# Issuing each unit's value product half a unit later in a hashed-attention kernel with two feed-forward layers behind it

## The chip, the cores and the metric

The program runs on one core of one Trainium2 chip. The metric is device time in microseconds (us), the median of several executions; less is better. Six queues matter: PE (TensorE's matmuls, in the order of the program), DVE (VectorE), ACT (ScalarE), POOL (GpSimd), and SP, which issues the DMAs. Each engine runs its own instructions in a fixed order and waits on semaphores for the others.

## The reference

Three steps follow each other: an attention whose mask is a hash (a query sees only the keys in its bucket), a feed-forward layer with an ELU, and one with a squared ReLU.

```python
def _attn_ref(q, k, v, proj):                 # B=2, H=8, S=768, D=64
    ...
    mask = q_bucket[:, :, :, None] == k_bucket[:, :, None, :]
    scores = scale * np.matmul(q, k.transpose(0, 1, 3, 2))
    scores = np.where(mask, scores, -1000000000.0)
    scores = scores - np.max(scores, axis=-1, keepdims=True)
    attn = np.exp(scores)
    attn = attn / (np.sum(attn, axis=-1, keepdims=True) + 1e-09)
    return np.matmul(attn, v).astype(np.float32)

def _moe_ref(x, w_in, w_out):                 # 1536 x 512, d_ff = 2048
    h = x @ w_in
    g = np.where(h > 0.0, h, alpha * (np.exp(np.minimum(h, 0.0)) - 1.0))
    return (g @ w_out).astype(np.float32)

def _moe2_ref(x, w_in, w_out, s, b):
    h = x @ w_in
    r = np.maximum(h, 0.0)
    return ((s * (r * r) + b) @ w_out).astype(np.float32)
```

The weights arrive in 64-bit floats; the kernel takes them apart into pairs of 16-bit parts itself.

## The kernel before

**Units.** The attention is 96 units: batch b, chunk c of 128 queries (6 per batch), head h (8 per chunk), in this order, so that units 0 to 47 are batch 0. A unit u is a chain over all engines, and the text calls its links by these names:

- scores S(u), `u_s`, line 358: 4 matmuls on PE (128 x 768 scores in two 16-bit parts) into one of two PSUM buffers;
- softmax, `u_soft`: DVE clamps and takes the maximum (line 368), POOL (units 16 to 43) or DVE scales it (line 369), ACT takes the exponential (line 370);
- split, `u_split`: ACT copies the probabilities to 16 bits (line 389, tile ph), POOL subtracts for the low part (line 392), and SP issues a DMA that transposes both parts (line 394, pt<-ph);
- value product A(u), `u_av`, line 412: 18 matmuls on PE from the transposed tile pt into xacc.

After the eighth head of a chunk `u_norm` divides by the sum (DVE, lines 426 to 430), and a transposing DMA puts the chunk into x for the first layer. Units 0 to 15 go another way (a transpose on PE, line 379); the change doesn't reach them.

**Layers.** The first layer works through six blocks of 256 tokens: `up` (h, 16 times 12 matmuls of 128x256, line 531) and `down` (x2p, 4 times 48). Behind each h tile come an exponential on ACT (e, line 539), DVE steps (e, g, lines 546 and 548), a copy on ACT (gh, line 551) and a subtraction on POOL (gl, line 554). While it runs, its weights are still being taken apart: DVE joins words (lines 194 to 197, wa), ACT rounds (wih, then woh, line 188), DVE subtracts for the low part (wil, wol, line 204). Then the second layer follows: `up2` (h) and `down2` (y, line 775).

**Order.** Between matmul groups the first layer hands out credit, and for each half of 2.5 us (1.2 us at first) the generator `attention` moves on to its next yield, which is half a unit. One round of its loop issues the split of the unit before, then A(u), then S of the unit `lag` later (4 units, PT = 4 buffers for pt, later 5), yields, then issues the softmax and what `sched` holds for that unit (the loads and hash bits of batch 1 from unit 41 on), and yields again. So A(u) and S(u+4) stand together, and the layer's products stand on either side. What the program writes is a priority, not the last word: the framework's scheduler places each instruction on its engine's queue by its own timeline, so that the final order differs a little from the written one. Rings bound the chain: 3 buffers for the exponentials, 3 for ph, 4 for pt.

At the boundary of the batches (units 41 to 50) the keys and queries of batch 1 are split (line 260), transposed, hashed on PE (pbit, line 320), compared on DVE (bits, line 323), and their buckets made on PE (pone, line 333) and written by ACT (line 337); the values are split by ACT (line 303) and DVE (vv, line 304).

Of the kernel before, what the change touches and what calls it, by code (L numbers as in the profile page):

```python
# [18 lines left out]
PT = 4  # L19
# [48 lines left out]
def model_kernel(tc, q, k, v, proj, w_in, w_out, w_in2, w_out2, s2, b2, sel, pop, eye, out):  # L68
    nc = tc.nc
    B, H, S, D = q.shape  # L70
    NB = proj.shape[1]
    DM, DFF = w_in.shape
    C = S // 128
# [3 lines left out]
    NU = B * C * H  # L77
# [15 lines left out]
    with ExitStack() as base:  # L93
# [248 lines left out]
        U0 = BLOCKS1[0] * H  # L342

        def unit(u):
            b, r = divmod(u, C * H)
            c, h = divmod(r, H)
            return b, c, h, h // 2, h % 2

        sps, pf, pt, sums, xacc = ({} for _ in range(5))
# [12 lines left out]
        def u_soft(u):  # L362
            b, c, h, hp, j = unit(u)
            if h == 0:
                sums[b, c] = sml.tile([128, H], F32, tag="sum", name="sum")
            f = ring.take("p", [128, S], F32, "p")
            mx = sml.tile([128, 1], F32, tag="mx", name="mx")
            nc.vector.tensor_scalar(f, sps.pop(u), CLAMP, None, op0=ALU.min, op1=ALU.min, accum_out=mx)  # L368
            (nc.gpsimd if U0 <= u < MXP else nc.vector).tensor_scalar(mx, mx, sm / (SQ * SQ), 10.0 * LN2, op0=ALU.mult, op1=ALU.add)  # L369
            nc.scalar.activation(out=f, in_=f, func=ACTF.Exp, scale=-sm / (SQ * SQ), bias=mx,  # L370
                                 accum_out=sums[b, c][:, h:h + 1])
            pf[u] = f

        def u_split(u, eng):
            f = pf.pop(u)
            if u < FC * H:
                p = ps_p[0].tile([128, S], F32, tag="s", name="pT")
                for cc in range(C):
                    nc.tensor.transpose(p[:, 128 * cc:128 * cc + 128], f[:, 128 * cc:128 * cc + 128], ident)  # L379
                o = ring.take("pt", [128, S], F32, "pt")  # L380
                if eng == "act":
                    nc.scalar.activation(out=o, in_=p, func=ACTF.Copy)
                else:
                    nc.vector.tensor_copy(out=o, in_=p)
                pt[u] = o
                return
            t = ring.take("ph", [128, 2, S], F16, "ph")
            if eng == "act":
                nc.scalar.activation(out=t[:, 0, :], in_=f, func=ACTF.Copy)  # L389
            else:  # L390
                nc.vector.tensor_copy(out=t[:, 0, :], in_=f)
            nc.gpsimd.tensor_tensor(out=t[:, 1, :], in0=f, in1=t[:, 0, :], op=ALU.subtract)  # L392
            o = ring.take("pt", [128, 2 * C, 128], F16, "pt")
            nc.sync.dma_start_transpose(out=o, in_=t.rearrange("p x s -> p (x s)"))
            pt[u] = o

        def u_av(u):
            b, c, h, hp, j = unit(u)
            if h == 0:
                xacc[b, c] = ps_x.tile([128, H, D], F32, tag="x", name="xacc")  # L400
            acc = xacc[b, c][:, h, :]
            o = pt.pop(u)
            if u < FC * H:
                vv = raws[b, hp, "v"].rearrange("p h (c d) -> p h c d", d=D)
                for cc in range(C):
                    nc.tensor.matmul(acc, o[:, 128 * cc:128 * cc + 128], vv[:, j, cc, :],  # L406
                                     start=(cc == 0), stop=(cc == C - 1))
                return
            vv = vHL[b, hp]
            for z, (x, y) in enumerate(((0, 0), (0, 1), (1, 0))):  # L410
                for cc in range(C):
                    nc.tensor.matmul(acc, o[:, C * x + cc, :], vv[:, j, cc, y, :],  # L412
                                     start=(z == 0 and cc == 0), stop=(z == 2 and cc == C - 1))
# [9 lines left out]
        def u_norm(b, c):  # L423
            sm_, acc = sums.pop((b, c)), xacc.pop((b, c))
            rs = sml.tile([128, H], F32, tag="rs", name="rs")
            nc.vector.tensor_scalar(rs, sm_, 1e-9 * SPR, (1.0 if b * C + c < FC else SV) / SX, op0=ALU.add, op1=ALU.mult)
            rr = sml.tile([128, H, 1], F32, tag="rr", name="rr")
            nc.vector.reciprocal(out=rr, in_=rs.rearrange("p (h o) -> p h o", o=1))
            xf = ring.take("p", [128, H, D], F32, "xf")
            nc.vector.tensor_tensor(out=xf, in0=acc, in1=rr.to_broadcast([128, H, D]), op=ALU.mult)  # L430
            xh = per.tile([128, 2, H * D], F16, tag="xh", name="xh")
            fl = xf.rearrange("p h d -> p (h d)")
            if FC <= b * C + c < C:
                nc.scalar.activation(out=xh[:, 0, :], in_=fl, func=ACTF.Copy)
            else:
                nc.vector.tensor_copy(out=xh[:, 0, :], in_=fl)
            nc.gpsimd.tensor_tensor(out=xh[:, 1, :], in0=fl, in1=xh[:, 0, :], op=ALU.subtract)
            ch = b * C + c
            nc.sync.dma_start_transpose(out=xx[ch // 4][:, :, ch % 4 * 128:ch % 4 * 128 + 128], in_=xh.rearrange("p x d -> p (x d)"))
# [27 lines left out]
        done_chunks = [0]  # L467
        in_done = [0]
        nxt = {"s": 0, "av": 0, "soft": [], "split": [], "lag": LAG0}

        def may_step():
            u = nxt["av"]
            return u >= NU or blk_of[u // H][0] < in_done[0] + XB

        def attention():
            for i in range(-PRE, 0):
                for fn, a in sched.get(i, []):
                    fn(*a)
                yield
            while nxt["av"] < NU:  # L480
                if nxt["split"]:
                    u_split(nxt["split"].pop(0), SPLIT(nxt["s"]))
                u = nxt["av"]
                if u < nxt["s"] and u in pt and (nxt["s"] - u >= nxt["lag"] or nxt["s"] == NU):
                    u_av(u)
                    nxt["av"] += 1
                    if u % H == H - 1:
                        b, c, *_ = unit(u)
                        u_norm(b, c)
                        done_chunks[0] = b * C + c + 1  # L490
                u = nxt["s"]
                if u < NU and u - nxt["av"] < nxt["lag"]:
                    if u == U0:
                        ring.use(p=[unp], ph=[un3], pt=[ptp])
                        nxt["lag"] = PT
                    u_s(u)
                    nxt["s"] += 1
                    yield
                    u_soft(u)
                    nxt["split"].append(u)  # L500
                    for fn, a in sched.get(u, []):
                        fn(*a)
                yield
        att = attention()


# [473 lines left out]
```

## Time and profile before

| | us |
|---|---|
| median of 3 runs | 713.86 |
| the runs | 713.5 to 716.53 |
| the profiled execution, its own time | 715.27 |
| its span in the trace | 713.5 |
| PE busy | 659.6 (92%) |
| DVE busy | 516.6 (72%) |
| ACT busy | 417.2 (58%) |
| POOL busy | 272.7 (38%) |

The page divides the span in forty slices of 17.8 us. The first 75 us hold the hash bits of batch 0 and the first units, with PE often waiting. From 98 us on the first layer runs beside the attention; the last value product is at 397 us. Second-layer products begin at 476 us. PE's busy time counts pipelined matmuls, so a busy PE isn't a PE at its peak; what it waits for is read from the idle time in square brackets in front of an instruction in the timeline, with the name of what ended it.

### The profile page before, as it was taken

The page shows a single profiled execution, that of the slowest core. Times are in us where ns is not written, and L with a number is a line of the kernel's source. Part 1 is how long each engine was busy: PE and PEld are TensorE (multiplying, and loading weights), DVE is VectorE, ACT ScalarE, POOL GpSimd, SP SyncE. Part 2 cuts the span into 40 slices and gives each one's busy share as a digit, 9 for nine tenths or more (in the row PEclk, how much of TensorE's full clock was granted, in tenths as well). Part 3 has the DMA queues.
Part 4 walks back from the last instruction along what each step waited for, and adds up shares of the span by engine and source line. Part 5 has one row for each costly group of instructions (what it writes and reads, how often), then busy time and mean ns, then how long its engine had stood idle before and what let it go on. Part 6 is the DMA issues. An engine that isn't in the chain of part 4 may idle for free.

```text
span 713.5 us, 15214 instructions
## 1 busy us (share of the span) xinstructions
PE 659.6 (92%) x6192; PEld 504.0 (71%) x6192; DVE 516.6 (72%) x885; ACT 417.2 (58%) x687; POOL 272.7 (38%) x219
## 2 busy tenths in 40 slices
PE   2789869888887999999999999999999999999998
PEld 0368657676666777888888988874444446888887
DVE  5688899888878468645744699439999726999730
ACT  2897679874797887756755333234555525555520
POOL 1257778873445278945854421311211200000000
PEclk9999979999999999999999999999999999999999
DMA  9984599999899588966768545004453000000100
GB/s 234 259 222 135 159 223 225 205 229 219 178 208 215 88 142 159 154 119 123 123 112 120 132 153 175 1 25 125 121 149 115 0 1 1 16 30 32 45 30 30
DMA packets 206742, 89.73 MB, mean 126 GB/s; under 512 B 171856, under 2 KB 203344, under 8 KB 206672
## 3 DMA queue, kind: packets, MB, share of 16 engines
q1 hardware_dynamic: 206080, 88.63, 56.4%
q8 instruction: 48, 0.79, 0.5%
q10 hardware_dynamic: 592, 0.14, 0.1%
q14 instruction: 22, 0.18, 0.1%
HBM read 43.13 MB, written 3.15 MB: 65 GB/s over the span
## 4 chain that ended last, share of the span: by engine, by line
PE 59%; DMA 11%; ACT 10%; DVE 7%; issue 6%; POOL 5%; SPq 0%; DVEq 0%; ACTq 0%; POOLq 0%
PE h L531 24%; PE y L775 15%; PE x2p L531 10%; DMA pt<-ph 6%; PE s L358 4%; POOL ph L392 3%; ACT p L370 3%; PE xacc L412 3%; ACT ph L389 2%; PE xacc L406 1%; DVE e L546 1%; DMA k<-src 1%; ACT gh L551 1%; PE pT L379 1%; DVE p L368 1%
## 5 line engine op out<-in xcount | busy, mean ns | idle before, releaser
L392 POOL TENSOR_TENSOR ph<-p,ph 128x768 f16<-128x768 f32 x80 | 133.9, 1679 | 65.3 <-ACT ph L389 45.7
L531 PE MATMUL h<-x,wih 128*128 128x256 f16 x768 | 132.5, 276 | 0.1
L531 PE MATMUL h<-x,wi 128*128 128x512 f16 x576 | 124.5, 379 | 0.0
L368 DVE TENSOR_SCALAR_CACHE_REDUCE p<-s 128x768 f32<-128x768 f32 x96 | 91.0, 950 | 44.4 <-PE s L358 42.1
L370 ACT ACTIVATE p<-p,mx 128x768 f32<-128x768 f32 x96 | 89.1, 928 | 46.4 <-DVE mx L369 40.5
L775 PE MATMUL y<-wqh,a 128*128 128x256 f16 x672 | 110.3, 273 | 0.0
L775 PEld LDWEIGHTS <-a 128*128 128x128 f16 x1008 | 98.5, 98 | 11.8
L531 PE MATMUL x2p<-gh,woh 128*128 128x256 f16 x384 | 104.8, 274 | 2.0 <-ACT woh L188 1.0
L531 PE MATMUL x2p<-gh,wol 128*128 128x256 f16 x384 | 105.0, 274 | 1.5 <-DVE wol L204 1.5
L531 PE MATMUL h<-x,wil 128*128 128x256 f16 x384 | 106.0, 276 | 0.0
L531 PE MATMUL x2p<-gl,woh 128*128 128x256 f16 x384 | 104.9, 274 | 0.5 <-POOL gl L554 0.4
L531 PEld LDWEIGHTS <-wi 128*128 128x128 f16 x576 | 56.3, 98 | 67.8
L775 PE MATMUL y<-wql,a 128*128 128x256 f16 x336 | 91.2, 273 | 0.0
L358 PE MATMUL s<-k,q 128*128 128x512 f16 (+1 forms) x384 | 81.0, 336 | 4.8 <-DVE p L368 4.5
L531 PEld LDWEIGHTS <-woh 128*128 128x128 f16 x768 | 74.8, 98 | 13.5 <-ACT woh L188 1.4
L531 PEld LDWEIGHTS <-wih 128*128 128x128 f16 x768 | 75.2, 99 | 12.8 <-issue 0.5
L554 POOL TENSOR_TENSOR gl<-g,gh 128x512 f16<-128x512 f32 x48 | 58.1, 1211 | 63.3 <-ACT gh L551 62.7
L412 PE MATMUL xacc<-vv,pt 128*128 128x64 f16 x1440 | 57.7, 195 | 18.2 <-DMA pt<-ph 18.2
L412 PEld LDWEIGHTS <-pt 128*128 128x128 f16 x1440 | 53.9, 99 | 24.3 <-DMA pt<-ph 21.2
L389 ACT ACTIVATE ph<-p 128x768 f16<-128x768 f32 x80 | 66.6, 836 | 5.2 <-DMA pt<-ph 4.1
L567 DVE SCALAR_TENSOR_TENSOR g<-h,sbs,r 128x512 f32<-128x512 f32 x48 | 35.7, 745 | 23.6 <-ACT r L564 23.6
L564 ACT ACTIVATE r<-h 128x512 f32<-128x512 f32 x48 | 28.2, 590 | 39.5 <-PE h L531 39.5
(121 smaller groups left out, 1043.3 us busy)
## 6 DMA issues: line engine op xcount, KB each, us to landing
wraw<-in_moe_w_in SPq DMA_DIRECT2D x32, 512.0 KB, 3.8
wraw<-in_moe_w_out SPq DMA_DIRECT2D x32, 512.0 KB, 3.9
out<-y SPq DMA_DIRECT2D x10, 256.0 KB, 2.0
raw<-in_k SPq DMA_DIRECT2D x6, 384.0 KB, 4.4
raw<-in_q SPq DMA_DIRECT2D x6, 384.0 KB, 4.4
v<-in_v SPq DMA_DIRECT2D x4, 384.0 KB, 5.1
pt<-ph SPq DMA_TRANSPOSE x80, 4.0
x<-in_k SPq DMA_DIRECT2D x2, 384.0 KB, 5.0
```

Source lines behind the costliest of these rows:

```text
L358: nc.tensor.matmul(p[:, a0:a1], w[b, hp][:, j, c, :], kf[:, a0:a1], start=(x == 0), stop=(x == 1))
L368: nc.vector.tensor_scalar(f, sps.pop(u), CLAMP, None, op0=ALU.min, op1=ALU.min, accum_out=mx)
L370: nc.scalar.activation(out=f, in_=f, func=ACTF.Exp, scale=-sm / (SQ * SQ), bias=mx, accum_out=sums[b, c][:, h:h + 1])
L379: nc.tensor.transpose(p[:, 128 * cc:128 * cc + 128], f[:, 128 * cc:128 * cc + 128], ident)
L389: nc.scalar.activation(out=t[:, 0, :], in_=f, func=ACTF.Copy)
L392: nc.gpsimd.tensor_tensor(out=t[:, 1, :], in0=f, in1=t[:, 0, :], op=ALU.subtract)
L412: nc.tensor.matmul(acc, o[:, C * x + cc, :], vv[:, j, cc, y, :], start=(z == 0 and cc == 0), stop=(z == 2 and cc == C - 1))
L531: nc.tensor.matmul(p, ws[a](kk), xs[b](kk), start=(kk == 0 and z == 0), stop=(kk == n_kk - 1 and z == 2))
L554: nc.gpsimd.tensor_tensor(out=gl, in0=t["g"], in1=gh, op=ALU.subtract)
L564: nc.scalar.activation(out=t["r"], in_=p, func=ACTF.Relu, scale=UN)
L567: nc.vector.scalar_tensor_tensor(out=g, in0=p, scalar=sb["s"], in1=t["r"], op0=ALU.mult, op1=ALU.mult)
L775: nc.tensor.matmul(p, a[:, xa, kk, :], wq[y][:, WQ[n], kk, :], start=first and k == 0, stop=k == 3 * K2 - 1, skip_group_check=True)
```

## The change

From unit 20 on (`U0 + PT`) the call that issues A(u) moves from in front of S to behind the first yield. Its condition is unchanged, but S is now issued first, with one unit more allowed between the two. So where the lag is 4, S(u+4) comes first, then half a unit of layer products, then A(u). Where the lag has become 5 (from about unit 40), A(u) now follows S(u+4) by half a unit, while before it stood in front of S(u+5).

```diff
+        def value():
+            u = nxt["av"]
+            if u < nxt["s"] and u in pt and (nxt["s"] - u >= nxt["lag"] or nxt["s"] == NU):
+                u_av(u)
+                nxt["av"] += 1
+                if u % H == H - 1:
+                    b, c, *_ = unit(u)
+                    u_norm(b, c)
+                    done_chunks[0] = b * C + c + 1
+
...
-                u = nxt["av"]
-                if u < nxt["s"] and u in pt and (nxt["s"] - u >= nxt["lag"] or nxt["s"] == NU):
-                    u_av(u)
-                    nxt["av"] += 1
-                    if u % H == H - 1:
-                        b, c, *_ = unit(u)
-                        u_norm(b, c)
-                        done_chunks[0] = b * C + c + 1
+                after = nxt["s"] >= U0 + PT
+                if not after:
+                    value()
                 u = nxt["s"]
-                if u < NU and u - nxt["av"] < nxt["lag"]:
+                if u < NU and u - nxt["av"] < nxt["lag"] + after:
...
                     u_s(u)
                     nxt["s"] += 1
                     yield
+                    if after:
+                        value()
                     u_soft(u)
...
+                elif after:
+                    value()
                 yield
```

No instruction is added or removed on any engine; all that changes is the order. The scheduler's answer shows on every engine at once.

On PE, at units 34 and 38. Before, the last rows of A(34) (its value tile is vv_878) stand in front of the scores S(38):

```order
L412 LDWEIGHTS pt
L412 MATMUL xacc<-vv_878,pt 128x64
L358 LDWEIGHTS q_373
L358 MATMUL s<-k_317,q_373 128x512
L358 LDWEIGHTS q_373
L358 MATMUL s<-k_317,q_373 128x256
```

After, S(38) and S(39) come first (here the last rows of S(39)), then four products of the first layer's `down`, then the first rows of A(34):

```order
L358 LDWEIGHTS q_375
L358 MATMUL s<-k_318,q_375 128x256
L540 LDWEIGHTS wol
L540 MATMUL x2p<-gh,wol 128x256
L540 LDWEIGHTS woh
L540 MATMUL x2p<-gh,woh 128x256
L540 LDWEIGHTS woh
L540 MATMUL x2p<-gl,woh 128x256
L540 LDWEIGHTS wol
L540 MATMUL x2p<-gh,wol 128x256
L412 LDWEIGHTS pt
L412 MATMUL xacc<-vv_878,pt 128x64
```

Two score groups have moved ahead of the value product. Counted in matmuls between S(34) and A(34), the unit has 13 layer products more in between.

On ACT, at units 39 and 40, where the last weight chunks of the first layer are due. Before, after the exponential and 16-bit copy of unit 39, those of unit 40 stand in front of five roundings of woh:

```order
L370 ACTIVATE p,sum<-p,mx 128x768
L389 ACTIVATE ph<-p 128x768
L370 ACTIVATE p,sum<-p,mx 128x768
L389 ACTIVATE ph<-p 128x768
L188 ACTIVATE woh<-wa 128x4x128 x5
L260 ACTIVATE src<-x_115 128x12x64
```

After:

```order
L370 ACTIVATE p,sum<-p,mx 128x768
L389 ACTIVATE ph<-p 128x768
L370 ACTIVATE p,sum<-p,mx 128x768
L188 ACTIVATE woh<-wa 128x4x128
L389 ACTIVATE ph<-p 128x768
L188 ACTIVATE woh<-wa 128x4x128 x4
L260 ACTIVATE src<-x_115 128x12x64
```

One rounding of woh has gone ahead of the copy of unit 40.

On DVE, at unit 49, in the boundary of the batches: the third of batch 1's four comparisons (bits) and two subtractions for the values (vv). Before:

```order
L326 COPY k_2852<-k_2852 64x768
L304 SCALAR_TENSOR_TENSOR vv_2930<-x_115,vv_2930 128x12x64
L304 SCALAR_TENSOR_TENSOR vv_3026<-x_115,vv_3026 128x12x64
L323 TENSOR_SCALAR bits<-pbit 128x768
L368 TENSOR_SCALAR p,mx<-s 128x768
```

After:

```order
L326 COPY k_2870<-k_2870 64x768
L304 SCALAR_TENSOR_TENSOR vv_2948<-x_115,vv_2948 128x12x64
L323 TENSOR_SCALAR bits<-pbit 128x768
L304 SCALAR_TENSOR_TENSOR vv_3044<-x_115,vv_3044 128x12x64
L368 TENSOR_SCALAR p,mx<-s 128x768
```

The comparison has gone ahead of one subtraction.

Three smaller moves of the same kind: on ACT the 16-bit copy of unit 29 stood in front of the exponential e of the seventh h tile and now stands behind it; on DVE one low-part subtraction of the weights (wol) now stands in front of the normalization of chunk 2 (xf), which waits for A(23); and between S(61) and A(61) there are 34 layer products fewer than before, and one value product and one and a quarter score groups fewer. From S(71) on the engines' queues hold the same sequence but for the place of the value products.

## Rows read from the trace of the kernel before

**Rows 1.** Page: span, then busy time, share and instructions of each engine.

```profile
span 713.5 us, 15214 instructions
...
PE 659.6 (92%) x6192; PEld 504.0 (71%) x6192; DVE 516.6 (72%) x885; ACT 417.2 (58%) x687; POOL 272.7 (38%) x219
```

**Rows 2.** Windows: stretch, length, busy (instructions) of PE, PEld, DVE, ACT, POOL, clock, DMA, GB/s.

```profile
98.00:130.00 32.00, 28.75 (x343) 23.40 (x342) 30.18 (x53) 29.25 (x54) 26.05 (x24) 0.93 1.09 230
...
160.00:183.00 23.00, 20.47 (x239) 16.87 (x238) 19.88 (x35) 11.27 (x19) 7.02 (x8) 1.00 0.87 203
183.00:250.00 67.00, 57.62 (x647) 44.50 (x645) 46.89 (x82) 55.44 (x91) 31.18 (x22) 0.97 0.91 174
250.00:300.00 50.00, 48.36 (x623) 40.40 (x622) 37.69 (x82) 40.82 (x75) 41.69 (x29) 1.00 0.93 152
300.00:400.00 100.00, 99.80 (x1251) 86.25 (x1250) 53.76 (x114) 59.40 (x100) 59.09 (x41) 1.00 0.68 117
```

**Rows 3.** Waits of PE: line, for what: us in total, times, longest.

```profile
PE xacc L412 <- DMA pt<-ph: 18.2, 14, 3.9
```

**Rows 4.** Timeline of PE, A(23), A(26), A(34): start, us, what, idle before.

```profile
119.67 0.70 PE L412 MATMUL xacc<-vv,pt 128*128 128x64 f16 x18 [1.13 <-DMA pt<-ph]
...
128.39 1.09 PE L412 MATMUL xacc<-vv,pt 128*128 128x64 f16 x18 [1.94 <-DMA pt<-ph]
...
156.45 0.70 PE L412 MATMUL xacc<-vv,pt 128*128 128x64 f16 x18 [1.98 <-DMA pt<-ph]
```

**Rows 5.** Timeline of ACT: unit 29's copy, and the seventh h tile's exponential.

```profile
130.18 0.83 ACT L389 ACTIVATE ph<-p 128x768 f16<-128x768 f32 x1
133.38 0.60 ACT L539 ACTIVATE e<-h 128x512 f32<-128x512 f32 x1 [2.37 <-PE h L531]
```

**Rows 6.** Timeline of DVE: unit 38's clamp, two wol subtractions, unit 41's clamp.

```profile
157.93 0.96 DVE L368 TENSOR_SCALAR_CACHE_REDUCE p<-s 128x768 f32<-128x768 f32 x1 [1.45 <-PE s L358]
...
168.70 1.77 DVE L204 SCALAR_TENSOR_TENSOR wol<-wa,woh 128x512 f16<-128x512 f32 x1 [2.05 <-ACT woh L188]
...
177.20 0.69 DVE L204 SCALAR_TENSOR_TENSOR wol<-wa,woh 128x512 f16<-128x512 f32 x1
...
180.73 0.96 DVE L368 TENSOR_SCALAR_CACHE_REDUCE p<-s 128x768 f32<-128x768 f32 x1
```

**Rows 7.** Timeline: ACT (unit 40's copy, one woh), then POOL (units 26 and 40).

```profile
167.30 0.84 ACT L389 ACTIVATE ph<-p 128x768 f16<-128x768 f32 x1 [1.39 <-DMA pt<-ph]
168.05 0.61 ACT L188 ACTIVATE woh<-wa 128x512 f16<-128x512 f32 x1
...
120.68 1.65 POOL L392 TENSOR_TENSOR ph<-p,ph 128x768 f16<-128x768 f32 x1 [1.47 <-ACT ph L389]
...
168.28 1.64 POOL L392 TENSOR_TENSOR ph<-p,ph 128x768 f16<-128x768 f32 x1 [1.71 <-ACT ph L389]
```

**Rows 8.** Timeline: DVE (two vv), then PE (pone, A(49)).

```profile
226.73 3.27 DVE L304 SCALAR_TENSOR_TENSOR vv<-x,vv 128x768 f16<-128x768 f32 x2
...
230.93 0.80 PE L333 MATMUL pone<-bits,sel_sb 128*128 128x512 f16 x2 [2.33 <-DVE bits L323]
...
242.56 0.52 PE L412 MATMUL xacc<-vv,pt 128*128 128x64 f16 x12 [0.85 <-DMA pt<-ph]
```

**Rows 9.** Timeline: A(61) on PE, unit 61's subtraction on POOL; then landings of all pt.

```profile
283.68 0.69 PE L412 MATMUL xacc<-vv,pt 128*128 128x64 f16 x18
...
277.25 1.66 POOL L392 TENSOR_TENSOR ph<-p,ph 128x768 f16<-128x768 f32 x1
...
DMA to landing us min/median/max: 3.6/4.0/6.8
```

**Rows 10.** Chain that ended last, 302 to 307 us: start, us, what.

```profile
302.81 2.62 PE x2p L531 x24
305.43 0.53 PE xacc L412 x18
305.96 0.65 PE s L358 x4
```

## The prediction

> **What bounds the kernel now.** I read the page's busy times first, then busy time by stretch, then PE's waits, then single instructions. PE is busy for 92% of 713.5 us [rows 1]. From 300 us on it is full: 99.80 of 100 us [rows 2], and a steady unit costs what its matmuls cost, 2.62 us for 24 layer products (0.109 each), 0.53 for a value product and 0.65 for scores [rows 10]. The change alters no instruction, so nothing can be won there; a microsecond won before 300 us should arrive at the end whole, and one lost too. What can be won is PE's idle time before that. The wait the change aims at, value products for their transposed tile, is 18.2 us in 14 waits [rows 3]. Its longest, 3.9 us, belongs to A(17), which like A(16) stands ahead of the first layer product in both orders. So at most 18.2 - 3.9 = 14.3 us can be reached.
>
> These waits lie in stretches with different limits. From 98 to 130 us DVE is busy for 30.18 of 32 us and ACT for 29.25; from 160 to 183 DVE for 19.88 of 23, with PE idle for 2.53; from 183 to 250 PE is idle for 9.4 of 67 us and ACT busy for 55.44; from 250 to 300 PE is idle for 1.64 of 50 [rows 2]. Only part of a wait removed on PE comes through where DVE or ACT is the one that has no time.
>
> **The change, part by part.**
>
> *98 to 130 us: nothing.* A(23) waits 1.13 us and A(26) 1.94 us [rows 4]. By the order A(23) comes seven layer products later, so 7 x 0.109 = 0.76 of its wait is filled. But the next tile, that of A(26), lands when its chain is through, not when PE is ready: its POOL subtraction starts at 120.68, behind a wait for ACT's copy [rows 7]. Nothing of that chain is moved. Between S(26) and A(26) PE's order adds one product. What A(23) gives, A(26) takes; I count 0.
>
> A rule speaks against the change here. The wol subtraction at 168.70 lasted 1.77 us with POOL's subtraction running since 168.28; the one at 177.20, with POOL idle, took 0.69 [rows 6, 7]. The Trainium skill (SBUF — State Buffer, "SBUF: two separate sides") says that a VectorE operation with two SBUF inputs and a GpSimd operation that reads SBUF take a shared port pair as an exclusive lock, and the later one waits for the whole of the earlier; the two rows look like it. In the new order one wol stands ahead of the normalization of chunk 2, about where unit 26's subtraction begins. By the rule that subtraction, and A(26) behind it, would come up to 0.7 us later, and the gain below would be 3.5 instead of 4.2. I leave it out of the sum: which of the two starts first is a matter of tenths.
>
> *130 to 157 us: -1.1.* ACT idles for 2.37 us ahead of the exponential at 133.38, because that waits for the h tile behind A(26); unit 29's copy (0.83 us) was done just ahead of that idle time [rows 5]. In the new order the copy stands behind the exponential, so ACT does it after the wait instead of before, and the copies behind it, those of units 30 to 34, are about 0.83 us later. Against this, A(34) waits 1.98 us [rows 4] and now has 13 products (1.42 us) more between its scores and itself. It can fill its 1.98 us and the lost 0.83 only in part by products, but two score groups (1.30 us) have also moved from behind it to ahead of it. I take -1.98 + 0.83 = -1.15, say -1.1. The bounds are 0 (ACT's delay reaches A(30) and A(31), which have no slack, and is paid twice) and -1.98.
>
> *157 to 183 us: another -2.5.* DVE's clamp of unit 38 waits 1.45 us for S(38), which stands behind A(34) [rows 6]. With S(38) in front of A(34), I take 0.9 of that. Then comes the largest single piece. At 168.70 DVE waits 2.05 us for a woh [rows 6], and that woh (0.61 us, at 168.05) stands on ACT behind unit 40's copy, which itself waits 1.39 us for a DMA [rows 7]. The new order puts the woh ahead of the copy: it is ready while ACT is idle, and DVE's 2.05 us go. The wol behind it also leaves the place where it took 1.77 instead of 0.69 us, another 1.08. So unit 41's clamp, at 180.73 the end of a row of weight operations on DVE, comes 0.9 + 2.05 + 1.08 = 4.0 us earlier, and with it the batch boundary, which starts from there. PE can follow by its own 1.1 plus the 2.53 us that it idles in this stretch waiting for weights: 3.6. The smaller counts: -3.6 at 183 us, of which 2.5 arise here. Bounds: the 2.05 us alone, or all of 4.0.
>
> *183 to 250 us: -1.6.* PE waits 2.33 us for bits at 230.93, and DVE spends the 3.27 us from 226.73 on two subtractions vv just ahead of them [rows 8]. One of the two (half of 3.27, 1.63) now comes behind the comparison. The next wait of PE, 0.85 us at A(49) [rows 8], sets a cap, since its tile lands no earlier; but by the order PE has thirteen layer products (1.42 us) and four bucket matmuls more between S(49) and A(49), so that about 1.6 us get through. Others here gain and lose by tenths: A(41) has five products fewer, A(44) fourteen more. I take -1.6; bounds 0 and -1.6 - 0.85 = -2.45. Below that lies one thing more: the clock. It reads 0.97 over these 67 us [rows 2], which is some 4 us at 1.2 instead of 2.4 GHz, a loss of 0.03 x 67 = 2.0 us, and those slow matmuls stand right behind the wait at 230.93 (two of them 0.80 us long [rows 8]). If the shorter wait no longer brings the clock down, up to 2.0 us come back. I keep this for the lower end.
>
> *250 to 300 us: +1.0.* Here the lag is 5 and the change brings A forward by half a unit. For units 56 to 61 that matters. Between S(61) and A(61) there are 34 products, a value product and one and a quarter score groups fewer: 34 x 0.109 + 0.53 + 0.82 = 5.1 us. Unit 61's tile is subtracted from 277.25 to 278.91, and a landing takes 4.0 us, so it is there at about 282.9, and A(61) starts at 283.68 [rows 9]: a slack of 0.8. The chain itself gets earlier too, since on POOL one layer subtraction no longer stands between units 60 and 61 and on DVE the clamp's successors come sooner; I put that at 3 us and the price at 5.1 - 0.8 - 3 = 1.3, less what PE wins by not waiting at unit 62, so 1.0. Bounds: 0 and 5.1 - 0.8 = 4.3.
>
> *300 to 397 us: nothing.* A comes half a unit (12 products, 1.31 us) earlier behind its scores. The chain from scores to landing is some 9 us and the distance 16, so there is cover.
>
> *Sum:* -3.6 - 1.6 + 1.0 = -4.2 us. The profiled execution took 715.27, so it would be 711.1; it lies 1.4 above the median of the runs, and against that median, 713.86, the forecast is **709.7 us**.
>
> **The rivals.**
>
> *More comes through.* The gains take their outer bounds and the late price is 0: -3.6 - 2.45 - 2.0 = -8 us, **706**. For it: the clock's loss stands right behind a wait that shrinks. Against it: a wait that shrinks is usually met by the next chain, as at A(26).
>
> *Nothing arrives.* The distance between scores and values is set by the scheduler, and the count says that it grows for units 23 to 52 by 0.4 us on average and shrinks later. If DVE and ACT, at 91 to 94% in the first stretch, set the pace, the waits only move, the woh gain (2.05 us) is met by a late copy of unit 40, and the late price takes the rest: -1.1 - 1.6 + 1.0 to 0, **712 to 714**.
>
> *Slower.* The tiles of units 60 and 61 become the bound: PE reaches A(61) 5.1 us sooner by its order, and the tile is no earlier, because ACT's exponential of unit 61 or POOL's subtraction isn't. Then A(61) waits 4.3 us, and PE, full from there on, never makes it good. It decides for slower once the gain ahead of it is under 0.7 us, thus only along with a batch boundary that starts as late as before: 713.86 + 4.3 = **718**. For it: a slack of only 0.8 us. Against it: that all of it happens on engines that have more idle time than before 183 us.
>
> **How the numbers follow.** The forecast and its neighbourhood (708 to 711.5) have 0.42, more comes through 0.14, nothing arrives 0.26, slower 0.18. A change of 0.5%, 3.6 us, is about what a measurement of this kernel can tell from no change; the line is at 710.3. Faster by more than that: 0.14 and two thirds of 0.42, 0.42. Within it: the other third and nearly all of 0.26, 0.40. Slower: 0.18. The range has 706 from the first rival at the lower end; the upper end is 715.2, where the late price of 4.3 us comes in full on a gain of 3.0 us, and leaves the slower case out.
>
> **What would show it.** Right: in the trace of the changed kernel A(16), A(17) and A(26) wait about as long as before, DVE's clamp of unit 38 hardly waits, the 2.05 us for woh are gone and unit 41's clamp starts near 177, pone waits under 1 us, and PE is full from 296 us on. Wrong: unit 41's clamp still at 180, which kills 2.5 of the 4.2 us; a new wait of over 1.5 us at A(30) or A(31), which means that ACT's moved copy costs more than A(34) gives; or one of over 2 us at A(60) or A(61). The whole argument falls if PE isn't full after 300 us.

## The result: slower by about half a per cent

| | us |
|---|---|
| before, median (20 runs beside it) | 713.85 (711.14 to 716.53) |
| after, median (20 runs) | 717.93 (714.33 to 724.08) |
| ratio after / before | 1.0059, 95% interval 1.0044 to 1.0075 |
| forecast | 709.7 (706.0 to 715.2) |
| profiled execution of after, its own time | 714.33 (span 712.5) |

Two later comparisons of the same pair gave 1.0046 (1.0028 to 1.0065) and 1.0047 (1.0025 to 1.0069). So the change costs 3.3 to 4.2 us where 4.2 were to be won. The profiled execution is the fastest of the twenty, 3.6 us under their median: what follows from its rows is the mechanism, and not the whole size of the loss.

**The profile after.** The page's first lines, as in [rows 1]:

```profile
span 712.5 us, 15215 instructions
PE 658.9 (92%) x6192; PEld 503.3 (71%) x6192; DVE 516.5 (72%) x885; ACT 416.1 (58%) x687; POOL 269.3 (38%) x219
```

The windows of [rows 2] (columns as there):

```profile
98.00:130.00 32.00, 28.72 (x346) 23.58 (x345) 31.48 (x53) 28.06 (x53) 25.71 (x24) 0.93 1.10 217
160.00:183.00 23.00, 20.54 (x238) 16.53 (x236) 18.62 (x32) 10.75 (x19) 6.25 (x8) 1.00 0.88 199
183.00:250.00 67.00, 59.13 (x665) 46.02 (x663) 47.16 (x83) 55.06 (x90) 31.15 (x22) 0.97 0.94 174
...
300.00:400.00 100.00, 98.88 (x1229) 85.26 (x1228) 49.16 (x114) 57.48 (x99) 58.67 (x41) 1.00 0.72 117
```

PE has gained 1.5 us between 183 and 250, and lost 0.9 after 300, where it was full before. The wait that the change aims at, and PE's timeline at A(23), A(26), A(31), A(34), the third pone of batch 1 and A(94):

```profile
PE xacc L412 <- DMA pt<-ph: 16.4, 15, 3.9
```

```profile
118.52 0.70 PE L412 MATMUL xacc<-vv,pt 128*128 128x64 f16 x18 [1.02 <-DMA pt<-ph]
126.72 1.14 PE L412 MATMUL xacc<-vv,pt 128*128 128x64 f16 x18 [2.02 <-DMA pt<-ph]
146.46 0.70 PE L412 MATMUL xacc<-vv,pt 128*128 128x64 f16 x18 [1.80 <-DMA pt<-ph]
157.55 0.70 PE L412 MATMUL xacc<-vv,pt 128*128 128x64 f16 x18 [1.60 <-DMA pt<-ph]
...
228.73 0.80 PE L333 MATMUL pone<-bits,sel_sb 128*128 128x512 f16 x2 [2.32 <-DVE bits L323]
...
392.26 0.70 PE L412 MATMUL xacc<-vv,pt 128*128 128x64 f16 x18 [1.08 <-DMA pt<-ph]
```

18.2 us in 14 waits [rows 3] have become 16.4 in 15, but the two aren't alike: A(16)'s wait, 2.82 us before and 2.70 after, is put down to this DMA before and to DVE after. With it the changed kernel has 19.1 us in 16 waits, so in all they haven't shrunk. Those of A(23), A(26) and A(34) are nearly what they were [rows 4]; the largest new ones are at A(31) and A(94), which did not wait before. A(31) in the kernel before:

```profile
147.17 0.69 PE L412 MATMUL xacc<-vv,pt 128*128 128x64 f16 x18
```

Executions differ in their first 98 us by up to 3.2 us, ahead of the first changed instruction. So times are compared from the start of the first layer product on (97.93 us before, 96.47 after). The table has two profiled executions of the kernel before and three of the changed one; all work ahead of A(95) is the same in both.

| us after the first layer product | before | before, again | after | after, again | after, again |
|---|---|---|---|---|---|
| exponential of unit 31 (ACT) | 38.64 | 39.05 | 40.57 | 41.41 | 40.13 |
| A(31) | 49.24 | 49.59 | 49.99 | 51.24 | 49.38 |
| clamp of unit 41 (DVE) | 82.80 | 82.83 | 83.28 | 85.19 | 83.80 |
| third pone of batch 1 | 133.00 | 132.83 | 132.26 | 134.44 | 132.92 |
| A(95), the last value product | 299.46 | 299.24 | 300.36 | 302.44 | 300.87 |

Up to unit 41's clamp the changed kernel loses 0.5 to 2.4 us, to the third pone it wins 1.0 back (49.1 instead of 50.1 us between the two), and from there to A(95) it loses 1.6 (168.0 instead of 166.4).

### The profile page after: what moved, and what is told of

The parts are those of the page before. It is cut to its first block, busy times and chain, and to the rows that moved or that the text cites. A ratio compares the mean times of both kernels' runs of the same rounds, so it can differ in the third digit from the quotient of the medians.

```text
span 712.5 us, 15215 instructions
## 1 busy us (share of the span) xinstructions
PE 658.9 (92%) x6192; PEld 503.3 (71%) x6192; DVE 516.5 (72%) x885; ACT 416.1 (58%) x687; POOL 269.3 (38%) x219
## 4 chain that ended last, share of the span: by engine, by line
PE 59%; DMA 13%; DVE 10%; ACT 8%; issue 6%; POOL 2%; SPq 1%; DVEq 0%; ACTq 0%; POOLq 0%
PE h L540 25%; PE y L784 15%; PE x2p L540 10%; DMA pt<-ph 7%; PE s L358 4%; PE xacc L412 3%; DVE p L368 2%; ACT p L370 2%; POOL ph L392 2%; ACT ph L389 1%; PE xacc L406 1%; DVE e L555 1%; DMA x<-xh 1%; DVE g L557 1%; ACT gh L560 1%
## 5 line engine op out<-in xcount | busy, mean ns | idle before, releaser
L412 PE MATMUL xacc<-vv,pt 128*128 128x64 f16 x1440 | 57.6, 195 | 19.5 <-DMA pt<-ph 16.4
L358 PEld LDWEIGHTS <-q 128*128 128x128 f16 x384 | 36.2, 100 | 24.0 <-issue 9.1
```

Of the source, the lines that this page charges most:

```text
L358: nc.tensor.matmul(p[:, a0:a1], w[b, hp][:, j, c, :], kf[:, a0:a1], start=(x == 0), stop=(x == 1))
```

## Experiments

All times are medians, each beside runs of the kernel before on the same chip (713.9 to 714.5); the numbers in the edits are the unit whose scores come next.

### Which half loses

Four kernels on one chip: the changed kernel once more, the change for units 20 to 39 alone, the change from unit 40 on alone, and the changed kernel with the whole distance of lag 5 given back late.

```diff
-                after = nxt["s"] >= U0 + PT
+                after = U0 + PT <= nxt["s"] < 40        # e2_early
+                after = nxt["s"] >= 40                  # e3_late
...
-(nxt["s"] - u >= nxt["lag"] or ...
+(nxt["s"] - u >= nxt["lag"] + (nxt["s"] > U0 + PT) or ...   # e4_full
```

> The changed kernel once more, for a second profiled execution, since the one at hand (714.33 us) is the fastest of twenty and the median is 717.93. Both theories: 716 to 720 us. Theory LATE (the 4 us come from units 40 to 95, where the value product stands half a unit nearer to its scores): a typical execution shows waits of 2 to 4 us more than before on transposed tiles behind 250 us. Theory EARLY (they come from units 20 to 40, where ACT's moved copies delay the tiles): a typical execution shows those 2 to 4 us between 98 and 183 us. Theory CLOCK: one or two more stretches at 1.2 GHz than the four of the kernel before.

> The change for units 20 to 39 alone: all engines have the changed order up to unit 43 or so and the order of before from there on. Theory LATE: 710 to 712 us, the early gain without the late loss. Theory EARLY: 717 to 718 us, the whole loss. Theory CLOCK: as EARLY if the added slow stretch stands before 250 us.

> The change from unit 40 on alone: the order of before up to unit 36 or so, the changed order from there on. Theory LATE: 717 to 718 us. Theory EARLY: 713 to 714 us, as before.

> The change for all units from 20 on, with the value product half a unit behind the scores of the unit five later once the lag is 5, so that no unit after 40 has its value product nearer to its scores than before (late distance 19.0 to 20.3 us of matmuls instead of 16.5 to 17.8 before and 15.2 to 16.5 in the change). Theory LATE: 710 to 713 us. Theory EARLY: 717 to 718 us.

Measured: the changed kernel 716.36, ratio 1.0046 (1.0028 to 1.0065); early alone 716.23, 1.0031 (1.0012 to 1.0051); late alone 716.02, 1.0019 (0.9999 to 1.0039); with the distance given back 716.46, 1.0033 (1.0012 to 1.0055). Neither half carries it (the late one alone can't be told from no change); the halves add up to 0.50%, the whole is 0.46%. The early half has a wait of 2.32 us at A(31) in its trace. With the distance given back A(94) doesn't wait any more, and A(31) still does (2.15 us).

### Which units, and what no change looks like

```diff
-                after = nxt["s"] >= U0 + PT
+                after = U0 + PT <= nxt["s"] < 28        # e5_20to27
+                after = nxt["s"] >= 28                  # e6_from28
+                after = 28 <= nxt["s"] < 92             # e7_28to91
```

e8_same is the kernel before without any edit.

> The change for units 20 to 27 alone (the rounds that issue scores 20 to 27); PE's order from unit 28 on is written as before. ACT's queue is nevertheless that of the changed kernel from unit 22 to unit 40 (unit 29's copy behind the exponential e of the 7th h tile, unit 30's exponential behind one more rounding of woh), as the scheduler's answer shows. Theory ACT (the loss of the early half is the wait of A(31), 1.8 to 2.3 us in the three profiles of the changed early order, which comes from ACT's moved copies, and the 1.2 GHz stretch behind it): all of the early loss is here, 716.0 to 716.5 against 713.9, A(31) waits 1.8 to 2.4 us. Theory PE (the loss comes from the places of the value products of units 28 to 39): 713.5 to 714.5, no wait at A(31). Theory NOISE (nothing but which execution one looks at): within 0.5 us of the unchanged kernel beside it.

> The change from unit 28 on. By the scheduler's answer ACT's queue is that of the kernel before up to unit 40, and A(34) and A(38) stand behind one score group more, all after unit 40 as in the changed kernel. Theory ACT: no wait over 0.6 us at A(31), no stretch at 1.2 GHz near 147 us, and the time is that of the change from unit 40 on or less: 713.0 to 715.5. Theory PE: 716 or more. Theory TAIL (A(94) waits 1 us because the distance at the end falls from 10.6 to 9.3 us): a wait of 0.5 to 1.2 us at A(94), which nothing gives back.

> The change for units 28 to 91: as from 28 on, but the last value products (of units 88 to 95) stand where they stood before. Theory TAIL: A(94) doesn't wait, and the time is 0.3 to 1.2 us below that of the change from 28 on: 712.5 to 714.5. If the wait of A(94) was no loss: the same time as from 28 on.

> The kernel before, unchanged, as if it were a change: what a comparison of this kind says of no change. Theory ACT and TAIL: a ratio within 0.0015 of 1, and a profile with stretches at 1.2 GHz near 90 and 128 us and none at 147 us; the one at 50 us, in which the profile first read lost 1.4 us, is not part of every execution. Theory NOISE: a ratio as far from 1 as 1.002 to 1.004, which would take the ground from under the halves.

Measured: 20 to 27 alone 715.78, 1.0023 (1.0007 to 1.0039), with 1.82 us at A(31); from 28 on 716.43, 1.0034 (1.0016 to 1.0052); 28 to 91 714.27, 1.0007 (0.9989 to 1.0025); no change 714.04, 0.9987 (0.9968 to 1.0006). So the early loss sits in the first rounds, and the second one in the last: the kernels from 28 on and 28 to 91 differ only in the value products of units 88 to 95, and by 0.27% (by the means of their runs 2.2 us, 95% interval 0.6 to 3.7). What is left in between can't be told from nothing. The theory ACT held for A(31) (no wait from 28 on) but missed the time of that kernel, which it put at 715.5 at most; the tail was larger than its wait in the traces.

### Mending both places

e9_copy29 takes unit 29's 16-bit copy away from ACT; e11_20to91 leaves the last rounds as before; e12_both does both. e10_fill26 is the kernel before with spare products in the wait ahead of A(26).

```diff
-                    u_split(nxt["split"].pop(0), SPLIT(nxt["s"]))
+                    u_split(nxt["split"].pop(0), "dve" if nxt["s"] == 30 else SPLIT(nxt["s"]))   # e9, e12
-                after = nxt["s"] >= U0 + PT
+                after = U0 + PT <= nxt["s"] < 92                                                # e11, e12
...
             vv = vHL[b, hp]
+            for _ in range({26: 20}.get(u, 0)):                                                 # e10
+                nc.tensor.matmul(acc, vv[:, j, 0, :, :].rearrange("p y d -> p (y d)"), vv[:, j, 0, 0, :], start=True, stop=True)
```

> The changed kernel, with unit 29's 16-bit copy on DVE instead of ACT. PE's order up to unit 33 is that of the changed kernel; on ACT the copy is gone from behind the exponential e of the 7th h tile, and unit 30's exponential stands ahead of the rounding of woh again. Theory ACT (A(31) waits because ACT is a copy of 0.83 us and a rounding of 0.6 us later with unit 30's exponential): A(31) waits under 0.9 us instead of 1.8 to 2.2, no 1.2 GHz stretch near 147 us, and the time falls by 1 to 2 us from that of the changed kernel, to 714.5 to 716. Theory PE (the places of the value products on PE make the wait): A(31) waits as before, 716 to 717, or more, since DVE pays for the copy.

> The kernel before, with 20 spare products of 128x64 (some 0.6 us) on PE ahead of S(30), within the 1.94 us for which PE waits for A(26); the spare products write a place that A(26) writes again from the start. Theory CLOCK (each stretch at 1.2 GHz behind a wait costs 1.0 to 1.7 us more): the stretch near 128 us is gone, and the time falls by 0.7 to 1.7 us, to 712.5 to 713.3. If the stretch stays, the same time or up to 0.6 us more. If the stretch goes and the time stays, the clock is no part of the loss.

> The changed kernel without its last rounds: for units 20 to 91, so that the value products of units 88 to 95 stand where they stood before. Theory TAIL (4.06 instead of 5.37 us between unit 94's transposing DMA and A(94), for a landing of 4.4 to 5.3 us): no wait at A(94), 0.5 to 2 us below the changed kernel, 714.5 to 716. If the tail is no loss: 716.4 and above.

> The changed kernel with both mends: unit 29's copy on DVE, and the change for units 20 to 91 alone. Theory ACT plus TAIL: the whole loss is gone, 713 to 714.5, and neither A(31) nor A(94) waits over 0.9 us. If a third cause holds: 715.5 or more. It is also the version that could beat both kernels, if units 32 to 60 give anything: then 712 to 713.

Measured: e9 716.1, 1.0026 (1.0005 to 1.0047); e10 715.26, 1.0007 (0.9984 to 1.0030); e11 715.87, 1.0027 (1.0008 to 1.0047); e12 715.39, 1.0016 (0.9999 to 1.0034).

e9 refutes the copy as the reason for the wait; its ratio lies below the change's 1.0046 to 1.0059, but the intervals overlap. The copy is gone from ACT, and A(31) waits longer than ever (PE's timeline, then ACT's up to unit 31's exponential, which is the last row):

```profile
147.01 1.11 PE L412 MATMUL xacc<-vv,pt 128*128 128x64 f16 x18 [2.75 <-DMA pt<-ph]
```

```profile
134.87 0.60 ACT L548 ACTIVATE e<-h 128x512 f32<-128x512 f32 x1 [0.63 <-PE h L540]
135.36 0.83 ACT L389 ACTIVATE ph<-p 128x768 f16<-128x768 f32 x1
136.10 0.62 ACT L560 ACTIVATE gh<-g 128x512 f16<-128x512 f32 x1
136.62 0.92 ACT L370 ACTIVATE p<-p,mx 128x768 f32<-128x768 f32 x1
```

The exponential of unit 31 still stands behind e of the 8th and gh of the 7th h tile. That is the late step, and not the copy that I had priced. The same stretch of ACT in the kernel before, and then in the changed one:

```profile
136.57 0.92 ACT L370 ACTIVATE p<-p,mx 128x768 f32<-128x768 f32 x1
137.49 0.62 ACT L551 ACTIVATE gh<-g 128x512 f16<-128x512 f32 x1
138.48 0.60 ACT L539 ACTIVATE e<-h 128x512 f32<-128x512 f32 x1 [0.37 <-PE h L531]
```

```profile
131.38 0.60 ACT L548 ACTIVATE e<-h 128x512 f32<-128x512 f32 x1 [2.03 <-PE h L540]
131.87 0.84 ACT L389 ACTIVATE ph<-p 128x768 f16<-128x768 f32 x1
...
135.30 0.60 ACT L548 ACTIVATE e<-h 128x512 f32<-128x512 f32 x1 [0.64 <-PE h L540]
135.79 0.83 ACT L389 ACTIVATE ph<-p 128x768 f16<-128x768 f32 x1
136.53 0.62 ACT L560 ACTIVATE gh<-g 128x512 f16<-128x512 f32 x1
137.04 0.92 ACT L370 ACTIVATE p<-p,mx 128x768 f32<-128x768 f32 x1
```

Before, unit 31's exponential (first row) runs ahead of gh and e; after, it is the last row behind both, and e waits for PE first. From the scores of unit 31 to its exponential it takes 3.4 us before (from 133.18 on) and 5.9 after (from 131.18 on). In e9 DVE, which now makes the copy, also brings unit 31's clamp later, 2.37 us behind its scores instead of 0.94; in e12 it comes after 1.10 us, and the exponential still 5.87 us behind the scores.

e10 tells nothing on the clock: with the spare products the queues moved, A(26) waited longer instead of shorter, and the stretch at 1.2 GHz stayed.

```profile
127.65 1.14 PE L414 MATMUL xacc<-vv,pt 128*128 128x64 f16 x18 [2.56 <-DMA pt<-ph]
```

e11 fits the tail theory. e12, at 715.4, is above the 713 to 714.5 that both mends were to give; its A(31) still waits 1.26 us, so the first mend was not one.

### The two places alone, and side by side

f1_tail has the order of before, and only at the end the distances of the changed kernel; f2_24to91 leaves out the first four rounds and the last; f3_after is the changed kernel again. g1, g2 and g3 repeat f2, e11 and f1 on one chip.

```diff
-                after = nxt["s"] >= U0 + PT
-                if not after:
+                after = nxt["s"] >= 88                          # f1, g3
+                if not after or nxt["s"] == 88:                 # f1, g3
...
+                after = 24 <= nxt["s"] < 92                     # f2, g1
```

> The kernel before up to unit 87, and from there the order of the changed kernel (one value product is issued twice as early once, so that A(84) to A(94) stand 1.31 us nearer their scores, as in the changed kernel; A(95) as before). Theory TAIL: these rounds alone cost what three pairs of kernels give for them, 0.19 to 0.27%, so 1.4 to 1.9 us, a ratio of 1.002 to 1.003, and A(94) waits 0.3 to 1.3 us in the profile. If the pairs were only scatter: a ratio within 0.001 of 1, or just the 0.3 to 0.7 us that the profiles mostly showed.

> The change for units 24 to 91. It differs from the change for units 20 to 91 (ratio 1.0027) by four rounds, those that issue scores 20 to 23; but by the scheduler's answer ACT's queue is then that of the kernel before, but for one neighbouring pair at unit 23, and unit 31's exponential stands ahead of e of the 8th and gh of the 7th h tile again. Theory ACT QUEUE (the early loss is the tile of unit 31, late because those two went ahead of its exponential): A(31) waits under 0.9 us, the ratio is that of the change for units 28 to 91, 0.999 to 1.001. If the early loss comes from the places of the value products on PE, most of which are still changed: 1.002 to 1.003.

> The changed kernel once more, beside the other two on the same chip: a third value for its ratio. Both theories: 1.004 to 1.006, the sum of the early part (0.2 to 0.25%) and the tail (0.19 to 0.27%), with waits at A(31) and A(94).

> The change for units 24 to 91 once more, beside the one for units 20 to 91, from which it differs by four rounds. Theory ACT QUEUE: 0.998 to 1.001, unit 31's exponential ahead of e and gh, A(31) waits under 0.9 us. Theory PE (the places of the value products): 1.002 to 1.003.

> The change for units 20 to 91 once more, on the same chip. Theory ACT QUEUE: 0.0015 to 0.0030 above the one for units 24 to 91 beside it, with A(31) waiting 1.5 to 2.6 us. Theory PE: the same ratio for the two.

> The last rounds alone once more. Theory TAIL: 1.001 to 1.003, and a wait of 0.3 to 1.3 us at A(94). If they cost nothing: 0.999 to 1.0005.

Measured:

| | median, us | ratio | 95% interval |
|---|---|---|---|
| f1, tail alone | 715.66 | 1.0014 | 0.9996 to 1.0032 |
| g3, tail alone | 716.79 | 1.0017 | 0.9997 to 1.0038 |
| f2, units 24 to 91 | 715.77 | 1.0009 | 0.9987 to 1.0031 |
| g1, units 24 to 91 | 714.83 | 1.0015 | 0.9990 to 1.0040 |
| g2, units 20 to 91 | 717.02 | 1.0034 | 1.0015 to 1.0053 |
| f3, the whole change | 717.90 | 1.0047 | 1.0025 to 1.0069 |

The four rounds that issue the scores of units 20 to 23 make 0.19% side by side (g2 and g1; by the means of their runs 1.9 us, 95% interval 0.1 to 3.8), and 0.18% by e11 and f2. They are the ones that turn ACT's queue. In the profiled executions, that of e10 apart, there is no overlap: in the nine whose ACT queue is that of before at this place, unit 31's exponential comes 3.38 or 3.39 us after its scores start, and A(31) waits 0 to 0.7 us; in the ten with those rounds it is 5.87 to 5.91 us, and A(31) waits 1.26 to 2.75. ACT in g1, from unit 31's exponential on, and PE's A(31) there, without a wait; then A(31) in g2:

```profile
135.43 0.92 ACT L370 ACTIVATE p<-p,mx 128x768 f32<-128x768 f32 x1
136.35 0.62 ACT L560 ACTIVATE gh<-g 128x512 f16<-128x512 f32 x1
137.34 0.60 ACT L548 ACTIVATE e<-h 128x512 f32<-128x512 f32 x1 [0.38 <-PE h L540]
```

```profile
146.59 0.69 PE L412 MATMUL xacc<-vv,pt 128*128 128x64 f16 x18
```

```profile
147.97 1.14 PE L412 MATMUL xacc<-vv,pt 128*128 128x64 f16 x18 [2.02 <-DMA pt<-ph]
```

The same rounds also move value products of units 18 to 37 and scores of units 32 to 41 on PE, and they turn POOL's queue at unit 23, which makes A(26) later (below). In the mean of the ten profiles A(31) comes 1.6 us later after the first layer product than in that of the nine (50.6 and 49.0), and 0.6 of it is there at A(26) already. So the wait at A(31) is shown to come with ACT's queue, and the whole 0.19% only with the rounds.

The tail alone costs 0.14 and 0.17%; each interval just reaches 1, the mean of the two (half-widths 0.18 and 0.20%, so about 0.13% together) doesn't: 1.0002 to 1.0029. A(94) in the kernel before, in f1 and in g3:

```profile
394.13 0.69 PE L412 MATMUL xacc<-vv,pt 128*128 128x64 f16 x18
```

```profile
394.01 0.70 PE L412 MATMUL xacc<-vv,pt 128*128 128x64 f16 x18 [0.55 <-DMA pt<-ph]
```

```profile
390.45 0.70 PE L412 MATMUL xacc<-vv,pt 128*128 128x64 f16 x18 [0.68 <-DMA pt<-ph]
```

A wait of 0.6 us is half of the 1.0 to 1.2 us of the ratios. From S(94) to A(95) it is more: 14.51 us before, 15.24 in f1 and 15.36 in g3, so 0.7 and 0.9 longer. Whether the rest is scatter or a longer landing in executions that were not profiled stays open. The early rounds (0.18 and 0.19%), the tail (0.14 and 0.17) and the middle (0.07, 0.09 and 0.15, none told from nothing) add up to 0.4 to 0.5%, against 0.46 to 0.59% for the whole; the first pairs gave more, 0.23% for the early rounds (e5) and 0.27 for the tail (e6 and e7). No version beat the kernel before.

## Why the prediction was wrong

**98 to 130 us, nothing: in truth 0.6 us lost.** In the profiled execution of after the forecast looks right: A(26) comes 30.25 us after the first layer product instead of 30.46, and waits 2.02 instead of 1.94 us. That was luck. Unit 26's tile landed there 5.46 us after its DMA was issued, and 5.78 to 6.03 us in the eighteen other profiles. In the mean of the ten profiles with the late exponential A(26) comes at 30.96 and waits 2.40 us, in that of the nine others at 30.34 and waits 1.89. "Nothing of that chain is moved" was the step that failed. On POOL a gl went ahead of unit 23's subtraction (before, then after):

```profile
110.67 1.97 POOL L392 TENSOR_TENSOR ph<-p,ph 128x768 f16<-128x768 f32 x1
112.60 1.16 POOL L554 TENSOR_TENSOR gl<-g,gh 128x512 f16<-128x512 f32 x1
```

```profile
109.31 1.16 POOL L563 TENSOR_TENSOR gl<-g,gh 128x512 f16<-128x512 f32 x1
110.44 1.64 POOL L392 TENSOR_TENSOR ph<-p,ph 128x768 f16<-128x768 f32 x1
```

Counted from the first layer product, unit 23's subtraction starts at 13.96 us instead of 12.74. There are three buffers for ph, so unit 26's copy on ACT waits until unit 23's tile has landed, 0.5 us longer than before (before, then after):

```profile
119.71 0.84 ACT L389 ACTIVATE ph<-p 128x768 f16<-128x768 f32 x1 [0.92 <-DMA pt<-ph]
```

```profile
118.56 0.84 ACT L389 ACTIVATE ph<-p 128x768 f16<-128x768 f32 x1 [1.45 <-DMA pt<-ph]
```

The delay of up to 0.7 us that I had weighed for unit 26's subtraction doesn't show: it starts 0.97 us behind the start of that copy before and after.

**130 to 157 us, -1.1: the main step that failed.** I priced one moved instruction on ACT, unit 29's copy at 0.83 us, and set its delay against A(34). The queue had turned at more places. What mattered was the exponential of unit 31, which lost its place to e and gh and came 1.9 us later (40.57 instead of 38.64). I had named A(30) and A(31) as without slack, and the bound that I put there, 0, was no bound: a chain that PE meets with so little slack (unit 31's tile landed 0.43 us ahead of A(31) before) hands on to PE what is left of its delay. The tile landed 1.13 us later (49.94 instead of 48.81), A(31) came 0.75 us later, and PE, which was ready sooner, waited 1.80. At A(34) it still waits 1.60. The 13 layer products that I counted between S(34) and A(34) aren't there either: by the order of the two traces there is one more, 64 instead of 63, and the two score groups, 1.41 us in all, which is 13 products' worth: I had counted the score groups twice. Two entries of my list of what would show me wrong came true: unit 41's clamp still at 180 (179.75), and over 1.5 us at A(31).

**What the clock adds.** It differs between executions of the same program. In the profiled execution of after the granted clock stays at 2.4 GHz behind A(31); in the repeat (e1) PE idles 2.22 us there and runs at 1.2 GHz behind it. Windows of the repeat ahead of and behind A(31), then PE's rows there:

```profile
144.10:147.50 3.40, 1.29 (x24) 0.76 (x20) 3.33 (x6) 2.37 (x4) 3.24 (x4) 1.00 1.18 280
147.50:150.90 3.40, 3.29 (x30) 2.62 (x31) 2.79 (x4) 2.07 (x3) 2.46 (x3) 0.50 0.92 214
```

```profile
147.61 1.14 PE L412 MATMUL xacc<-vv,pt 128*128 128x64 f16 x18 [2.22 <-DMA pt<-ph]
...
148.76 0.42 PE L540 MATMUL x2p<-gh,wol 128*128 128x256 f16 x1
148.97 0.42 PE L540 MATMUL x2p<-gh,woh 128*128 128x256 f16 x1
```

The products there start every 0.21 us instead of every 0.11. Up to A(31) the repeat is 1.25 us behind the other, at A(34) still 1.06, and at unit 41's clamp 1.9. A stretch at 1.2 GHz that begins between 146 and 161 us stands in seven of the ten profiles with the late exponential and in none of the nine others; in five of the seven it stands at A(31), in two at A(34). At half speed the second window's 3.4 us would be a loss of up to 1.7 us, but it doesn't show as one: in the five profiles PE doesn't wait at A(34) at all, where the other five with the late exponential wait 1.60 to 2.28 us, and A(34) follows A(31) by 10.8 to 11.0 us, in the other five by 11.1 to 11.8. The slower products fill a wait that stood behind them. What the clock adds to the loss isn't shown.

**157 to 183 us, another -2.5: failed.** In the profiled execution of after the clamp of unit 38 hardly waits, as forecast, and S(38) comes 1.5 us earlier (in the repeat 1.3 later). But the clamp of unit 40 waits 1.16 us instead, and unit 41's clamp is at 83.28, not 4.0 us ahead of 82.80. One woh went ahead of unit 40's copy, and the next one took its place behind it. ACT (the woh that went ahead, unit 40's copy, the next woh), then DVE's wol behind each woh, then POOL:

```profile
165.46 0.61 ACT L188 ACTIVATE woh<-wa 128x512 f16<-128x512 f32 x1
168.20 0.84 ACT L389 ACTIVATE ph<-p 128x768 f16<-128x768 f32 x1 [2.12 <-DMA pt<-ph]
168.95 0.61 ACT L188 ACTIVATE woh<-wa 128x512 f16<-128x512 f32 x1
```

```profile
166.11 0.69 DVE L204 SCALAR_TENSOR_TENSOR wol<-wa,woh 128x512 f16<-128x512 f32 x1 [0.54 <-ACT woh L188]
...
169.59 1.77 DVE L204 SCALAR_TENSOR_TENSOR wol<-wa,woh 128x512 f16<-128x512 f32 x1 [1.47 <-ACT woh L188]
```

```profile
169.17 1.64 POOL L392 TENSOR_TENSOR ph<-p,ph 128x768 f16<-128x768 f32 x1 [2.94 <-ACT ph L389]
```

DVE's wait of 2.05 us [rows 6] is now 0.54 and 1.47 us, 2.01 together, and the 1.77 us of the wol beside POOL's subtraction are back at one wol further on. I had followed the woh that moved, and not the one that stood behind the blocked copy afterwards: the copy waits for a DMA (2.12 us, 1.39 before [rows 7]), and whatever is next in ACT's queue waits with it. By unit 41's clamp these two parts were to have won 3.6 us; the three profiles of after are 0.5 to 2.4 us behind there.

**183 to 250 us, -1.6: right in sign, 1.0 in size.** The wait ahead of pone didn't shrink (2.32 us, 2.33 before): PE got there earlier too. And the one vv that stays ahead of the bits took 2.28 us, not half of the pair's 3.27 (DVE's vv, bits and the other vv, then POOL):

```profile
225.52 2.28 DVE L304 SCALAR_TENSOR_TENSOR vv<-x,vv 128x768 f16<-128x768 f32 x1
227.73 0.94 DVE L323 TENSOR_SCALAR bits<-pbit 128x768 f16<-128x768 f32 x1
228.60 1.73 DVE L304 SCALAR_TENSOR_TENSOR vv<-x,vv 128x768 f16<-128x768 f32 x1
```

```profile
225.24 1.75 POOL L392 TENSOR_TENSOR ph<-p,ph 128x768 f16<-128x768 f32 x1
```

POOL's subtraction ran from 225.24 to 226.99, and the vv ended 0.8 us after that, about what one takes alone in this trace (0.96 for the vv of 231.87). The Trainium skill (SBUF — State Buffer, "SBUF: two separate sides") has the later of two such operations wait for the whole of the earlier one. These rows and the wol above agree: 169.17 + 1.64 = 170.81, and that wol ends at 171.36, 0.55 later.

Part of the 1.0 goes back at once. The other vv now stands ahead of a clamp on DVE, and in two of the three profiles of after the fourth pone waits 1.0 us, which the profile puts down to that clamp; it waited in neither profile of before. In f3:

```profile
232.57 0.49 PE L333 MATMUL pone<-bits,sel_sb 128*128 128x512 f16 x2 [1.04 <-DVE p L368]
```

**250 to 397 us, +1.0: 1.6, at other places.** A(61) waits 0.27 us and not 4.3, although PE is there 3.8 us earlier (181.98 instead of 185.75 after the first layer product): the rival that ended near the measured time had the wrong place. Of the 1.6 us some 0.7 are lost between the third pone and S(94), the fourth pone's wait among them, and 0.8 behind it. That is the wait of A(94), in a stretch that I had called covered with "a distance of 16". That is the distance while score groups still come. At the end none follow: before, A(94) starts 11.26 us behind S(94), and the order takes 12 products, 1.31 us, out of that. The transposing DMA of unit 94 was issued 5.37 us ahead of A(94) before; by the order 4.06 remain, and from its issue to A(94) it took 5.30, 4.76 and 4.62 us in the three profiles of after. The 9 us that I gave the chain from scores to landing were too few as well: for unit 94 it took 10.5 us before.

**The sum.** Forecast -3.6 - 1.6 + 1.0 = -4.2. In the mean of the profiles it is +1.3 to unit 41's clamp, -1.0 to the third pone and +1.6 from there on, +1.9 in all: the three profiled executions are 1.0, 3.1 and 1.5 us behind those of before at A(95), and the timed runs 3.3 to 4.2. The term with the wrong sign is the first, the gain ahead of 183 us. The gap between 1.9, the mean of the three, and these isn't settled: profiled executions of the changed kernel lay 3.6, 0.3 and 3.1 us below the medians of its runs.

## What to carry to other kernels

When a change turns an engine's queue, compare the whole queue between the two places where it is the same again, and follow every chain that passes there: the delay belongs to the instruction that lost its place, not to the one that moved most visibly. Follow the buffers too: unit 26 was late because unit 23, three buffers ahead of it, was. An instruction moved out from behind a blocked one gains only if nothing takes its place. And read a distance at the end of a loop by itself, since what filled it in the middle no longer comes.

## What the runs showed of the hardware

PE's granted clock falls with a wait of 2 to 2.5 us in some executions and not in others of the same program: at A(26) the three profiled executions of the changed kernel waited 2.02, 2.47 (e1) and 2.54 us (f3), and the clock fell to 0.50 with the first two and stayed at 1.00 with the longest. And a landing is no constant: from the issue of unit 94's transposing DMA to A(94) it took 4.62 to 5.30 us in three executions of one program, the difference between a wait of 0.4 and one of 1.08 us.
